# Attention and two MLPs on one core: the order of the first transfers, and new prices for the planner

## The chip, the cores and the metric

The kernel runs on one core of a Trainium2 chip. The metric is the device time of one execution in microseconds. The core has a matrix engine (TensorE, called PE in the profile; its weight loads stand under PEld), a vector engine (VectorE, DVE), a scalar engine for activations (ScalarE, ACT), GpSimd (POOL), a sync engine that mostly issues transfers (SyncE, SP), and DMA queues that the engines fill. PE writes to PSUM banks; everything else lies in SBUF or in device memory.

## The reference

Four batches of eight heads, 576 tokens, head dimension 64. The attention output is the input of a first MLP, and that of a second, gated one. All arrays are float32, but the weights come to the chip as 64-bit floats. q, k and `w_gate` are drawn some six times larger than the other inputs, so the softmax is sharp and a coarse number format would show.

```
log_f = np.log(np.clip(f, 0.0001, 1.0));  cum = np.cumsum(log_f, axis=-1)
decay = cum[:, :, :, None] - cum[:, :, None, :]
scores = np.where(causal, -1000000000.0, scale * q @ k.T + decay)
attn = softmax(scores) @ v                          # 4 x 8 x 576 x 64
x = attn.transpose(0, 2, 1, 3).reshape(2304, 512)
h = x @ w_in                                        # 512 -> 2048
x = (h * np.tanh(np.log1p(np.exp(h)))) @ w_out      # -> 512
out = (sigmoid(x @ w_gate) * (x @ w_val)) @ w_out2  # 512 -> 1536 -> 512
```

## The kernel before

**Number formats.** The MLPs run in split fp16: a value is a high and a low half, and a product is three matmuls (high-high, high-low, low-high; lines 1114 to 1116 for `w_in`, 1165 to 1167 for `w_out`). A weight tile arrives as 512 KB of raw 64-bit words. `load_w` sends it (line 712), `float32` rebuilds float32 on DVE in three integer instructions of 128 x 512 (lines 662, 666, 670), `scaled` makes the high half on ACT (line 527) or DVE (line 530), and `low_part` the low half: on DVE (line 681), or on PE with two matmuls into a bank `w_ps` (lines 687 and 688) that ACT reads out (line 690). The first MLP has 32 such tiles, n = 0 to 31: two for `win0`, then `win1` and so on, with `wout0` and the rest among them. Raw words land in parts of `xt`, or, for tiles 2 and 3, in `win5` and `win4` (`XPLACE`).

**Start.** `decay` loads the gates `f` and a matrix `carry`, clips (line 471), takes the logarithm with a sum per row on ACT (line 473), runs a small Exp, so that the Exp table is loaded (line 474), adds up earlier segments with one matmul by `carry` (line 479), and scans (line 484). The running sums go as rows into the score operands (line 490): the row `rq` beside q on SP's queue, `rk` beside k on ACT's, each in two segments. `ones` puts the rows of constants beside them (lines 426 and 428): in a score product, a row of sums beside k meets a row of constants beside q, and the other way round. `constants` loads an identity (`eyes`).

**Attention.** The first 256 queries of batch 0 run in fp32, a pair of heads at a time, four pairs p: `scores_first` (line 821, into `s_ps`), a row maximum with the mask on DVE (line 756), Exp on ACT (line 808), a diagonal of reciprocals (line 530), transposes by matmul (`t_ps`, line 847), and the product with v (line 1011). All the rest of the attention has scores of 384 to 576 columns (lines 886, 891, 953), probabilities in two fp16 halves (`pp`, lines 527 and 764), transposes by DMA (line 930), and its product with v at line 1023.

**Steps.** The first MLP goes in steps: one step is a block of 256 tokens and a group g of 256 hidden columns. `h_stream` issues a step's h matmuls into one of three `h` banks, `mish` applies the activation on ACT and DVE, which frees the bank with the low half of g (line 1087), and `y_stream` adds g times `wout` into `y_ps`. Step 0 is the first block's group 0, step 7 its group 7.

**Order.** Nothing of the order is written by hand. All the pieces are coroutines; the class `Order` runs them as a list scheduler with a clock for each engine, estimated costs, and a due time for each piece. Prices (`P_DVE`, `P_ACT`, `P_POOL`, `P_PORT`, `TAU`, `NEAR`) decide between plans on different engines; numbers such as `MISH`, `PRE0`, `B0`, `VLATE` shift due times. What it yields is a fixed instruction list for each engine. Each engine runs its list in order and waits on semaphores. In gaps that the planner expects for PE it puts matmuls by the mask into a `y_ps` bank (`fill`, line 1129), which compute nothing that is used; there are 80 of them.

Of the kernel before, what the change touches and what calls it, by code (L numbers as in the profile page):

```python
# [11 lines left out]
ACTF = mybir.ActivationFunctionType  # L12
# [24 lines left out]
DMA_LAG = 2.007  # L37
# [2 lines left out]
WP0 = 0  # L40
SLACK = 0.571
SLACK_P = 3.484
NEAR = 0.092
P_DVE = 2.396
P_ACT = 3.156
P_POOL = 1.906
P_PORT = 7.287
P_EXP = 2
TAU = 28.792
LOAD0 = 0.5  # L50
FILL0 = 1.2
FILL = 0.7
# [10 lines left out]
class Order:  # L63
# [162 lines left out]
    def run(self):  # L226
        while True:
            self.unblock()
            best = None
            for e, ops in self.ops.items():  # L230
                if ops:
                    c = self.clock[e]
                    first = min(self.begin(t, c) for t in ops) + NEAR

                    ready = [t for t in ops if self.switch(t) and t["time"] < c - PATIENCE]
                    ready = ready or [t for t in ops if self.begin(t, c) <= first]
                    t = min(ready, key=lambda t: (t["due"], t["n"]))
                    start = self.begin(t, c)
                    if e == "SP" and len(t["req"]) > 2 and t["req"][1] < 1:

                        start = max(start, self.clock["DMA"] - DMA_QUEUE)
                    if best is None or start < best[0]:
                        best = start, e, t
            if best is None:
                break
            start, e, t = best
            cold = False
            if e == "PE":
                gap, busy = max(0.0, start - self.clock[e]), 0.0
                cold = self.warm * 2.0 ** (-gap / TAU_PE) < WARM  # L250
                if self.fill and gap > FILL_MIN:

                    share = FILL if self.n_fill else FILL0
                    busy = self.fill(int(share * gap / (FILL_US * (1 + cold)))) * FILL_US * (1 + cold)
                    self.n_fill += busy > 0
                    busy = min(busy, gap)
                self.warm *= 2.0 ** (-(gap - busy) / TAU_PE)
                self.warm = 1.0 - (1.0 - self.warm) * 2.0 ** (-busy / TAU_PE)
                cold = self.warm < WARM
            self.ops[e].remove(t)  # L260
            if self.switch(t):
                self.table = t["req"][2]
            _, us, *dma = t["req"]
            if e == "PE":
                us *= 1 + cold
                self.warm = 1.0 - (1.0 - self.warm) * 2.0 ** (-us / TAU_PE)
            if e != "SP":
                dma = ()
            self.use(e, start, us)
            if self.port(t["req"]):  # L270
                self.use("PORT", start, us)
            end = start + us
            if dma:
                t["time"] = end
                self.clock["DMA"] = end = max(self.clock["DMA"], end + 0.65) + dma[0] / DMA_RATE
                end += DMA_LAG
                if len(dma) > 1:
                    self.event[dma[1]] = end
                    self.changed = True
                else:  # L280
                    t["time"] = end
            elif e == "PE":

                t["time"], t["lag"] = end, self.AFTER[e]
            else:
                t["time"] = end + self.AFTER[e]
            self.step(t, None)
        assert not self.blocked, [(t["due"], t["req"]) for t in self.blocked]
# [39 lines left out]
def attention_moe_moe_kernel(ctx, tc, qk, v, f, carry, ident, const, rows_q, rows_k, w_in, w_out, w_gate, w_val, w_out2, out):  # L328
# [37 lines left out]
    def need(*keys):  # L366
        yield ("need", keys)
# [46 lines left out]
    Q32 = SAB.rearrange("p a q h s -> p a q (h s)").bitcast(FP32)  # L414

    def constants():
        yield "SP", 0.5, 131072, "eye"
        nc.sync.dma_start(out=eyes, in_=ident)
        od.due(0)
        yield "SP", 0.5, 10000, "cq"  # L420
        nc.sync.dma_start(out=SBt[67:KB], in_=rows_q)

    def ones():

        yield "SP", 0.5, 10000, "ones_k"
        nc.sync.dma_start(out=K32[64:65].rearrange("o a q s -> o (a q s)"), in_=const[0:1])
        yield "SP", 0.5, 10000, "ones_q"
        nc.sync.dma_start(
            out=Q32[65:KF].rearrange("o a q s -> o (a q s)"), in_=const[1:2, 0:2 * NPB * 320]
        )  # L430
        yield from need("ones_k", "ones_q")
        done("ones")
# [23 lines left out]
    def decay():  # L456
        ft = words(wout[NG1 - 1], 1536, 2 * SL).bitcast(FP32)
        cum = words(wout[NG1 - 2], 1536, 2 * SL).bitcast(FP32)
        c16 = words(win[NG1 - 2], 0, 3 * SL).rearrange("p (a s) -> p a s", a=3)
        zt = words(wout[0], 0, 2 * SL).bitcast(FP32)  # L460
        tot, car, tab = (words(wout[0], 2 * SL + 2 * k, 2).bitcast(FP32) for k in range(3))
        cm = words(wout[0], 512, 256).bitcast(FP32)
        yield "SP", 0.5, 74000, "gates"
        nc.sync.dma_start(out=ft, in_=f)
        yield "SP", 0.5, 65536, "carry"
        nc.sync.dma_start(out=cm, in_=carry)
        yield from need("gates")
        yield "DVE", t_dve2(SL) + 0.2
        nc.vector.memset(zt, 0.0)
        nc.vector.memset(tab, 0.0)  # L470
        nc.vector.tensor_scalar(ft, ft, 1.0e-4, 1.0, op0=ALU.max, op1=ALU.min)
        yield "ACT", t_act(SL, 0.28)
        nc.scalar.activation(out=ft, in_=ft, func=ACTF.Ln, accum_out=tot)
        nc.scalar.activation(out=tab, in_=tab, func=ACTF.Exp, scale=0.0)
        yield from need("carry")
        (hi,) = yield from take("h")
        hp = t_ps("h", "carry_ps")[:, 0:1]
        yield "PE", 0.3
        nc.tensor.matmul(hp, lhsT=cm, rhs=tot, start=True, stop=True)
        yield "DVE", 0.13  # L480
        nc.vector.tensor_copy(car, hp)
        give("h", hi)
        yield "DVE", t_dve(SL)
        nc.vector.tensor_tensor_scan(out=cum, data0=ft, data1=zt, initial=car, op0=ALU.add, op1=ALU.add)

        for seg in range(2):
            for row, key in ((Q32[64:65], "rq"), (K32[65:KF], "rk")):
                n = min(SL, 256 - seg * SL)
                yield "SP", 0.5, 10000, (key, seg)
                (nc.scalar if key == "rk" else nc.sync).dma_start(  # L490
                    out=row.rearrange("o a q s -> o (a q) s")[:, :, seg * SL:seg * SL + n],
                    in_=cum[seg * NH:seg * NH + 2 * NPB, 0:n],
                )
        od.due(-20)
        for seg in range(1, 4):
            yield "SP", 0.5, 5000, ("cum_f", seg)
            nc.sync.dma_start(out=cum_f[:, seg * SL:(seg + 1) * SL], in_=cum[seg * NH:seg * NH + 2 * NPB])
        spawn(first_rows(), -20)
        yield from need(*[("cum_f", seg) for seg in range(1, 4)])
        od.due(0)  # L500
        yield "DVE", 3 * t_dve(SL) + 3 * t_dve2(SL)
        for j in range(3):
            nc.vector.tensor_copy(c16[:, j], cum)
            if j < 2:
                nc.vector.tensor_tensor(cum, cum, c16[:, j], op=ALU.subtract)
        for seg in range(4):
            yield "SP", 0.5, 10000, ("cum", seg)
            nc.sync.dma_start(
                out=cum_d.rearrange("j b t p s -> (b t p) j s")[:, :, seg * SL:(seg + 1) * SL],
                in_=c16[seg * NH:(seg + 1) * NH],  # L510
            )
# [52 lines left out]
    def prep_first(p, part, turn):  # L564
# [2 lines left out]
        j = qi % NQ  # L567
        for c in ((0, 1), (2, 3, 4))[part]:
            qs_t[p, c] = (SA[j], SB[j], c * 128 - c0, qi)
        yield "SP", 0.68, 512 * n, ("k32", p, part)  # L570
        nc.sync.dma_start(out=K32[0:64, :, p, c0:c0 + n], in_=qk[p, 64:128, :, c0:c0 + n])
        yield "SP", 0.68, 512 * n, ("q32", p, part)
# [123 lines left out]
    def load_w(hi, lo, src, scale, key, n):  # L696

        if n:
            yield from need(("st", 0) if n == 1 else ("rk", 1))

        if n in XPLACE:
            yield from take(turn=("wr", n))
# [6 lines left out]
        if n < NFIRST:  # L709
            od.due((-49.95, -49.5, -28.8, -27.8)[n])  # L710
        yield "SP", 0.5, 128 * 4096
        (nc.scalar if n < 2 else nc.sync).dma_start(
            out=raw.rearrange("p n t -> p (n t)").rearrange("p (a n) -> p a n", a=src.shape[1]), in_=src
        )
        od.due(due)
# [1124 lines left out]


    LEAD = 1.91
    MISH = -1.309
    YDUE = 4.818
    SPAN = 6.867
    LATE = 0.504
    SPANA = 7.667
    C4 = 1
    PRE = 0.948
    PRE0 = -3.072  # L1850
    B0 = 9.728
    WIN = 6
    WOUT = -2
    VLATE = 5.624
    FIRST = ()
    NFIRST = 4
    XPLACE = {2: win[5], 3: win[4]}
# [2 lines left out]
    for b in range(NB):  # L1860
# [14 lines left out]
        for p in range(NPB):  # L1875
# [4 lines left out]
            if b == 0 and p == 3:  # L1880
                spawn(constants(), beg)
                spawn(masks(), beg)
                spawn(ones(), beg - 1)
        for p in range(NPB):
            spawn(prep_v(b, p, ("ld", nl)), beg + p - pre + 1)
            nl += 1
# [97 lines left out]
```

## Time and profile before

| | us |
|---|---|
| Runs | 908.98, 909.6, 910.5 |
| Median of the three | 909.6 |
| The profiled execution | 911.16 |
| Its span in the profile | 909.4 |
| PE busy in it | 896.6 (99%) |
| DVE busy | 714.8 (79%) |
| ACT busy | 551.3 (61%) |
| POOL busy | 19.2 (2%) |

The span runs from the first to the last instruction of the profiled execution; that execution's own time, 911.16 us, has some 1.8 us around it. PE counts as busy while any of its pipelined matmuls is under way, so its 99% includes matmuls at half clock and the fills. The mean granted clock of PE is 0.992 of full speed.

### The profile page before, as it was taken

The page shows a single profiled execution, that of the slowest core. Times are in us where ns is not written, and L with a number is a line of the kernel's source. Part 1 is how long each engine was busy: PE and PEld are TensorE (multiplying, and loading weights), DVE is VectorE, ACT ScalarE, POOL GpSimd, SP SyncE. Part 2 cuts the span into 40 slices and gives each one's busy share as a digit, 9 for nine tenths or more (in the row PEclk, how much of TensorE's full clock was granted, in tenths as well). Part 3 has the DMA queues.
Part 4 walks back from the last instruction along what each step waited for, and adds up shares of the span by engine and source line. Part 5 has one row for each costly group of instructions (what it writes and reads, how often), then busy time and mean ns, then how long its engine had stood idle before and what let it go on. Part 6 is the DMA issues. An engine that isn't in the chain of part 4 may idle for free.

```text
span 909.4 us, 21833 instructions
## 1 busy us (share of the span) xinstructions
PE 896.6 (99%) x8907; PEld 746.8 (82%) x8907; DVE 714.8 (79%) x1688; ACT 551.3 (61%) x1075; POOL 19.2 (2%) x32
## 2 busy tenths in 40 slices
PE   7999999999999999999999999999999999999998
PEld 6647788878887888878888887777888888888986
DVE  5999999888768875796799989999959556756634
ACT  4688688887767876585444455556655453554432
POOL 0000100010000000000100000000000000100000
PEclk7999999999999999999999999999999999999999
DMA  7688968668657773544344433301000100010010
GB/s 215 178 219 179 234 206 216 135 134 168 135 94 140 123 177 82 103 93 90 97 137 140 139 116 117 116 2 47 1 1 2 48 1 1 24 36 13 2 48 25
DMA packets 149431, 91.69 MB, mean 101 GB/s; under 512 B 103785, under 2 KB 132929, under 8 KB 149328
## 3 DMA queue, kind: packets, MB, share of 16 engines
q1 hardware_dynamic: 148466, 88.97, 40.4%
q8 instruction: 70, 1.15, 0.6%
q10 hardware_dynamic: 864, 1.32, 0.4%
q14 instruction: 31, 0.25, 0.1%
HBM read 51.38 MB, written 5.37 MB: 62 GB/s over the span
## 4 chain that ended last, share of the span: by engine, by line
PE 91%; DVE 6%; DMA 1%; issue 0%; ACT 0%; SPq 0%; POOL 0%; DVEq 0%; POOLq 0%; ACTq 0%
PE bank L1474 9%; PE bank L1473 9%; PE bank L1475 9%; PE h_ps L1114 7%; PE y_ps L1165 7%; PE y_ps L1166 7%; PE y_ps L1167 7%; PE h_ps L1115 7%; PE h_ps L1116 7%; PE o_ps L1023 4%; PE o_bank L1633 3%; PE o_bank L1634 3%; PE o_bank L1632 3%; PE o_acc L1798 2%; PE o_acc L1797 2%; PE o_acc L1796 2%
## 5 line engine op out<-in xcount | busy, mean ns | idle before, releaser
L1114 PE MATMUL h_ps<-xt,win 128*128 128x256 f16 x576 | 157.5, 273 | 0.1
L1115 PE MATMUL h_ps<-xt,win 128*128 128x256 f16 x576 | 157.1, 273 | 0.6 <-DVE sm L781 0.3
L1165 PE MATMUL y_ps<-g,wout 128*128 128x256 f16 x576 | 157.2, 273 | 0.0
L1116 PE MATMUL h_ps<-xt,win 128*128 128x256 f16 x576 | 157.1, 273 | 0.0
L1167 PE MATMUL y_ps<-g,wout 128*128 128x256 f16 x576 | 156.9, 272 | 0.0
L1166 PE MATMUL y_ps<-g,wout 128*128 128x256 f16 x576 | 156.9, 272 | 0.0
L756 DVE CUSTOM_DVE_ANT_0 sp<-s_ps,mask 128x384 f32<-128x384 f32 (+4 forms) x144 | 68.0, 493 | 22.6 <-PE s_ps L891 19.1
L1480 ACT ACTIVATE bank<-bank 128x512 f32<-128x512 f32 (+1 forms) x90 | 48.5, 539 | 61.2 <-PE bank L1475 60.3
L906 ACT ACTIVATE sp<-sp,sm 128x384 f32<-128x384 f32 (+3 forms) x112 | 63.8, 570 | 24.9 <-DVE sm L756 23.7
L764 DVE SCALAR_TENSOR_TENSOR pp<-sp,sm,pp 128x512 f16<-128x512 f32 (+4 forms) x128 | 76.5, 610 | 1.4
L1114 PEld LDWEIGHTS <-win 128*128 128x128 f16 x576 | 56.3, 98 | 13.2 <-issue 3.3
L1165 PEld LDWEIGHTS <-wout 128*128 128x128 f16 x576 | 56.3, 98 | 11.2 <-issue 2.0
L1115 PEld LDWEIGHTS <-win 128*128 128x128 f16 x576 | 56.4, 98 | 9.2 <-issue 1.5
L1077 ACT ACTIVATE h_ps<-h_ps 128x512 f32<-128x512 f32 x72 | 41.4, 582 | 36.5 <-PE h_ps L1116 36.1
L1087 DVE SCALAR_TENSOR_TENSOR g<-h_ps,g 128x512 f16<-128x512 f32 x72 | 49.2, 687 | 17.8 <-ACT g L1083 17.7
L1166 PEld LDWEIGHTS <-wout 128*128 128x128 f16 x576 | 56.3, 98 | 8.0
L1116 PEld LDWEIGHTS <-win 128*128 128x128 f16 x576 | 56.3, 98 | 7.5 <-issue 0.9
L1167 PEld LDWEIGHTS <-wout 128*128 128x128 f16 x576 | 56.3, 98 | 6.6
L1730 DVE TENSOR_TENSOR v<-bank,e 128x512 f32<-128x512 f32 (+1 forms) x30 | 19.1, 638 | 43.3 <-ACT bank L1480 42.6
L1646 DVE SCALAR_TENSOR_TENSOR xt<-o_bank,xt 128x512 f32<-128x512 f32 x42 | 28.5, 689 | 30.2 <-ACT o_bank L1480 22.0
L1083 ACT ACTIVATE g<-h_ps 128x512 f16<-128x512 f32 x61 | 36.2, 595 | 23.3 <-PE y_ps L1167 22.6
L1023 PEld LDWEIGHTS <-vt 128*64 128x64 f16 x1368 | 35.1, 110 | 14.2 <-issue 12.8
(298 smaller groups left out, 2492.2 us busy)
## 6 DMA issues: line engine op xcount, KB each, us to landing
xt<-w_out SPq DMA_DIRECT2D x16, 512.0 KB
xt<-w_in SPq DMA_DIRECT2D x12, 512.0 KB
wraw<-w_gate SPq DMA_DIRECT2D x12, 512.0 KB
wraw<-w_val SPq DMA_DIRECT2D x12, 512.0 KB
wraw<-w_out SPq DMA_DIRECT2D x12, 512.0 KB
vst<-v SPq DMA_DIRECT2D x12, 320.0 KB
st<-qk SPq DMA_DIRECT2D x12, 320.0 KB
st<-qk SPq DMA_DIRECT2D x12, 256.0 KB
```

The costliest lines, as they stand in the source:

```text
L756: nc.vector.tensor_tensor_reduce(out=sp, in0=ps_ap, in1=mk, op0=ALU.add, op1=ALU.min, scale=-0.125, scalar=1.0e38, accum_out=mn,)
L764: nc.vector.scalar_tensor_tensor(lo, a, scale, hi, op0=ALU.mult, op1=ALU.subtract)
L1023: nc.tensor.matmul(o_ps[64 * hh:64 * hh + 64, col:col + n], lhsT=vv[:, jc, vl, 64 * hh:64 * hh + 64], rhs=ptt[:, k, q0:q0 + n], start=(jc ...
L1114: nc.tensor.matmul(dst, lhsT=wh, rhs=xh, start=(k == 0), stop=False)
L1115: nc.tensor.matmul(dst, lhsT=wh, rhs=xl, start=False, stop=False)
L1116: nc.tensor.matmul(dst, lhsT=wl, rhs=xh, start=False, stop=(k == KD - 1))
L1165: nc.tensor.matmul(dst, lhsT=wh, rhs=gh, start=first, stop=False, skip_group_check=True)
L1166: nc.tensor.matmul(dst, lhsT=wl, rhs=gh, start=False, stop=False, skip_group_check=True)
L1167: nc.tensor.matmul(dst, lhsT=wh, rhs=gl, start=False, stop=last, skip_group_check=True)
L1473: nc.tensor.matmul(dst, lhsT=wh, rhs=xh[:, k], start=first, stop=False, skip_group_check=True)
L1474: nc.tensor.matmul(dst, lhsT=wh, rhs=xl[:, k], start=False, stop=False, skip_group_check=True)
L1475: nc.tensor.matmul(dst, lhsT=wl, rhs=xh[:, k], start=False, stop=last, skip_group_check=True)
```

## The change

The rows of constants (`ones`) go out first, and on ACT's queue. The first weight tile is sent only when the logarithm is issued (`need("ln")`); the second moves from ACT's queue to SP's, and waits, like all later ones, for the decay rows (`("rk", 1)`). `constants`, and the q and k of pairs 2 and 3, wait for the second segment of decay rows (`("rows", 1)`). The dummy Exp is issued behind the carry matmul in the program's text. Two transfers get a shorter estimated landing time, and nine of the planner's numbers are new.

```
-NEAR = 0.092
-P_DVE = 2.396
+NEAR = 0.098
+P_DVE = 2.413
...
-P_POOL = 1.906
-P_PORT = 7.287
+P_POOL = 1.759
+P_PORT = 6.132
...
-TAU = 28.792
+TAU = 19.169
...
     def constants():
+        yield from need(("rows", 1))
         yield "SP", 0.5, 131072, "eye"
...
     def ones():
-        nc.sync.dma_start(out=K32[64:65].rearrange("o a q s -> o (a q s)"), in_=const[0:1])
+        nc.scalar.dma_start(out=K32[64:65].rearrange("o a q s -> o (a q s)"), in_=const[0:1])
...
-        nc.sync.dma_start(
+        nc.scalar.dma_start(
             out=Q32[65:KF].rearrange("o a q s -> o (a q s)"), in_=const[1:2, 0:2 * NPB * 320]
         )
...
         nc.scalar.activation(out=ft, in_=ft, func=ACTF.Ln, accum_out=tot)
-        nc.scalar.activation(out=tab, in_=tab, func=ACTF.Exp, scale=0.0)
+        done("ln")
...
         nc.tensor.matmul(hp, lhsT=cm, rhs=tot, start=True, stop=True)
+        nc.scalar.activation(out=tab, in_=tab, func=ACTF.Exp, scale=0.0)
...
+            done(("rows", seg))
...
+        if p > 1:
+            yield from need(("rows", 1))
         yield "SP", 0.68, 512 * n, ("k32", p, part)
...
         if n:
-            yield from need(("st", 0) if n == 1 else ("rk", 1))
+            yield from need(("rk", 1))
+        else:
+            yield from need("ln")
...
-        (nc.scalar if n < 2 else nc.sync).dma_start(
+        (nc.scalar if n < 1 else nc.sync).dma_start(
...
-    MISH = -1.309
+    MISH = -2.209
...
-    PRE0 = -3.072
-    B0 = 9.728
+    PRE0 = -1.767
+    B0 = 10.922
...
-    VLATE = 5.624
+    VLATE = 0
...
-                spawn(ones(), beg - 1)
+                spawn(ones(), -49.96)
```

On ACT, the first instructions before: `xt_74` and `xt_73` hold the raw words of tiles 0 and 1, `wout_91` the gates, `wout_90` the running sums, `xt_75` the rebuilt float32, `win_76` the two halves of `win0`.

```order
L712 DMA xt_74<-w_in 128x2x512
L473 ACT_TABLE_LOAD
L473 ACTIVATE wout_91,wout_84<-wout_91 128x144
L474 ACT_TABLE_LOAD
L474 ACTIVATE wout_84<-wout_84 128x1
L712 DMA xt_73<-w_in 128x2x512
L490 DMA mab<-wout_90 1x8x144
L527 ACTIVATE win_76<-xt_75 128x512
L490 DMA mab<-wout_90 1x8x112
L527 ACTIVATE win_76<-xt_75 128x512
```

The same place of the changed kernel:

```order
L427 DMA mab<-const 1x4608
L429 DMA sab<-const 1x2560
L474 ACT_TABLE_LOAD
L474 ACTIVATE wout_91,wout_84<-wout_91 128x144
L481 ACT_TABLE_LOAD
L481 ACTIVATE wout_84<-wout_84 128x1
L719 DMA xt_74<-w_in 128x2x512
L492 DMA mab<-wout_90 1x8x144
L492 DMA mab<-wout_90 1x8x112
L815 ACTIVATE wout_88,sm<-wout_88,sm 128x128 x2
```

The rows of constants stand first, tile 0 stands where tile 1 stood, the two decay rows follow each other, and the high halves of `win0` are no longer ahead of the first Exp of the softmax.

On DVE, from the scan of the running sums to the first softmax instruction (`ISA`), before:

```order
L484 SCALAR_TENSOR_TENSOR wout_90<-wout_91,wout_84 128x144
L662 TENSOR_SCALAR xt_75<-xt_74 128x512
L666 SCALAR_TENSOR_TENSOR xt_75<-xt_74,xt_75 128x512
L670 SCALAR_TENSOR_TENSOR xt_75<-xt_74,xt_75 128x512
L681 SCALAR_TENSOR_TENSOR win_76<-xt_75,win_76 128x512
L662 TENSOR_SCALAR xt_75<-xt_73 128x512
L666 SCALAR_TENSOR_TENSOR xt_75<-xt_73,xt_75 128x512
L670 SCALAR_TENSOR_TENSOR xt_75<-xt_73,xt_75 128x512
L681 SCALAR_TENSOR_TENSOR win_76<-xt_75,win_76 128x512
L756 ISA wout_88,sm<-s_ps,mask 128x128
```

The same place of the changed kernel:

```order
L486 SCALAR_TENSOR_TENSOR wout_90<-wout_91,wout_84 128x144
L667 TENSOR_SCALAR xt_75<-xt_74 128x512
L671 SCALAR_TENSOR_TENSOR xt_75<-xt_74,xt_75 128x512
L675 SCALAR_TENSOR_TENSOR xt_75<-xt_74,xt_75 128x512
L533 TENSOR_SCALAR win_76<-xt_75 128x512
L686 SCALAR_TENSOR_TENSOR win_76<-xt_75,win_76 128x512
L763 ISA wout_88,sm<-s_ps,mask 128x128
```

Tile 1 has moved behind the softmax of all four pairs (before, three pairs stood in one piece), and the high half of tile 0 is made on DVE.

On PE, at the first product of low part `w_ps` for `win4` in the changed kernel, with the step that follows it (step 2, `win_78`):

```order
L1136 MATMUL y_ps<-mask 128x256
L893 MATMUL s_ps<-mab,sab 128x512
L692 MATMUL w_ps<-xt_75,eyes 128x512
L693 LDWEIGHTS eyes
L693 MATMUL w_ps<-win_80,eyes 128x512
L893 MATMUL s_ps<-mab,sab 128x384
```

In the kernel before, the low part for which PE waited is that for `win3`, and h matmuls of step 1 (`win_77`) follow it:

```order
L1129 MATMUL y_ps<-mask 128x256
L886 MATMUL s_ps<-mab,sab 128x384
L687 MATMUL w_ps<-xt_75,eyes 128x512
L688 LDWEIGHTS eyes
L688 MATMUL w_ps<-win_79,eyes 128x512
L1114 LDWEIGHTS win_77
```

In all, PE has 93 fills instead of 80 (18 and 21 around the carry matmul instead of 24 and 23) and eleven low parts instead of nine. ACT has 15 instructions fewer, and DVE some 16 more, most of them high halves. The first y step stands later in PE's list, and the low half of g of steps 0 and 4 later in DVE's.

## Rows read from the trace of the kernel before

**Rows 1.** The page, chain that ended last: shares of the span by engine.
```profile
PE 91%; DVE 6%; DMA 1%; issue 0%; ACT 0%; SPq 0%; POOL 0%; DVEq 0%; POOLq 0%; ACTq 0%
```

**Rows 2.** Windows: length; busy by PE, PEld, DVE, ACT, POOL; clock; DMA share; GB/s.
```profile
13.93:21.70 7.77, 7.77 (x27) 6.14 (x27) 4.76 (x30) 5.55 (x24) 0.00 (x0) 0.50 1.02 295
21.70:58.50 36.80, 33.49 (x238) 21.45 (x235) 36.19 (x107) 27.80 (x63) 0.00 (x0) 0.93 0.68 185
58.50:85.08 26.58, 26.47 (x202) 17.34 (x200) 24.79 (x65) 21.45 (x44) 0.00 (x0) 1.00 0.87 210
85.08:909.40 824.32, 819.83 (x8394) 694.78 (x8391) 642.66 (x1475) 492.08 (x941) 18.11 (x26) 1.00 0.38 91
```

**Rows 3.** Timeline, all engines, 0 to 14 us: start, duration, engine, line, [idle before].
```profile
1.42 5.30 PE L1129 MATMUL y_ps<-mask 128*128 128x256 bf16 x24 [1.42 <-POOL mask L436]
...
3.97 0.40 ACTq L712 DMA_DIRECT2D xt<-w_in  x1
...
4.39 1.28 ACT L474 ACT_TABLE_LOAD   x1
...
5.68 0.20 ACT L474 ACTIVATE wout<-wout 128x1 f32<-128x1 f32 x1
...
6.51 0.35 PE L479 MATMUL carry_ps<-wout 128*128 128x1 f32 x2
...
7.71 1.23 ACTq L490 DMA_DIRECT2D mab<-wout  x1
...
9.49 0.64 ACTq L490 DMA_DIRECT2D mab<-wout  x1
...
10.75 0.42 DVE L662 TENSOR_SCALAR xt<-xt 128x512 int32<-128x512 int32 x1
...
13.93 0.28 DVE L756 CUSTOM_DVE_ANT_0 wout<-s_ps,mask 128x128 f32<-128x128 f32 x1
```

**Rows 4.** Chain of the first 60 us, in order of time: start, duration, what.
```profile
9.74 2.95 DMA sab<-const
```

**Rows 5.** Timeline of PE, 12 to 86 us.
```profile
12.82 7.42 PE L821 MATMUL s_ps<-mab,sab 66*128 66x128 f32 x24 [3.43 <-DMA sab<-const]
...
25.59 1.48 PE L821 MATMUL s_ps<-mab,sab 66*128 66x128 f32 x8
...
50.43 1.53 PE L687 MATMUL w_ps<-xt,eyes 128*128 128x512 f32 x2 [1.96 <-DVE xt L670]
...
59.48 1.02 PE L687 MATMUL w_ps<-xt,eyes 128*128 128x512 f32 x2
60.34 0.38 PE L688 MATMUL w_ps<-win,eyes 128*128 128x512 f16 x1
60.55 0.27 PE L1114 MATMUL h_ps<-xt,win 128*128 128x256 f16 x1
60.66 0.27 PE L1115 MATMUL h_ps<-xt,win 128*128 128x256 f16 x1
...
85.08 0.27 PE L1114 MATMUL h_ps<-xt,win 128*128 128x256 f16 x1
```

**Rows 6.** Windows around the ends of two stretches at low clock.
```profile
23.00:24.00 1.00, 1.00 (x8) 0.85 (x6) 1.00 (x4) 0.00 (x0) 0.00 (x0) 0.65 1.00 371
...
52.00:54.00 2.00, 2.00 (x6) 0.85 (x4) 1.82 (x6) 1.64 (x6) 0.00 (x0) 0.50 0.95 351
...
55.00:58.00 3.00, 3.00 (x45) 1.87 (x40) 3.00 (x7) 2.62 (x7) 0.00 (x0) 1.00 0.50 169
```

**Rows 7.** Timeline of DVE near 51 us.
```profile
50.90 0.42 DVE L662 TENSOR_SCALAR xt<-xt 128x512 int32<-128x512 int32 x1
51.24 0.69 DVE L1087 SCALAR_TENSOR_TENSOR g<-h_ps,g 128x512 f16<-128x512 f32 x1
51.84 0.68 DVE L666 SCALAR_TENSOR_TENSOR xt<-xt,xt 128x512 int32<-128x512 int32 x1
52.44 0.55 DVE L756 CUSTOM_DVE_ANT_0 sp<-s_ps,mask 128x384 f32<-128x384 f32 x1
```

More of the change, by code (lines that the diff above doesn't have):

```diff
@@ L275, in run @@
                 self.clock["DMA"] = end = max(self.clock["DMA"], end + 0.65) + dma[0] / DMA_RATE
-                end += DMA_LAG
+                end += dma[2] if len(dma) > 2 else DMA_LAG
                 if len(dma) > 1:
@@ L462, in decay @@
         cm = words(wout[0], 512, 256).bitcast(FP32)
-        yield "SP", 0.5, 74000, "gates"
+        yield "SP", 0.4, 74000, "gates", 1.0
         nc.sync.dma_start(out=ft, in_=f)
-        yield "SP", 0.5, 65536, "carry"
+        yield "SP", 0.4, 65536, "carry", 1.0
         nc.sync.dma_start(out=cm, in_=carry)
```

## The prediction

> **What bounds the kernel now.** I read the chain that ended last first: 91% of it is TensorE (PE) and 6% VectorE (DVE) [rows 1]. Then the windows, cut at 85.08 us, where PE begins the sixth of the first MLP's h steps (step 5, counting from 0) [rows 2, 5]. Behind that cut PE is busy 819.83 of 824.32 us at a granted clock of 1.00, its level of 2.4 GHz: nothing but less PE work, or starting earlier, can shorten that part. Ahead of it PE is not the bound: between 21.7 and 58.5 us DVE is busy 36.19 of 36.80 us while PE is busy 33.49, part of it at the low clock, part with fill matmuls that compute nothing.
>
> So I keep one account: clock time minus useful PE work. Useful work is counted from the order of instructions, each kind with the distance of one start to the next: 0.11 us for an fp16 matmul of 256 columns (60.55 to 60.66), 0.86 for an fp32 one of 512 columns (59.48 to 60.34), so 0.65 for 384, 0.43 for 256 and 0.215 for 128, and 1.07 for a whole low part on PE (59.48 to 60.55) [rows 5]. Ahead of step 5 the kernel before has scores 17.2 us, transposes 5.0, attention times v 8.7, 120 h and 24 y matmuls 15.7, nine low parts 9.7: 56.3 us. **85.08 - 56.3 = 28.7 us have gone to other things** by then, and almost nothing is lost later. The change can only move this 28.7 and the useful total.
>
> The start, in the timeline [rows 3]: 24 fills run from 1.42 to 6.51, 0.212 us each. The carry matmul stands behind them; 1.20 us after it, at 7.71, the rows of the decay sum are sent. ScalarE (ACT) sends the second of its two at 9.49 only, because a conversion stands in between. The ones rows go last, at 9.74, and land 2.95 us later [rows 4]. DVE meanwhile converts two weight tiles, and the first softmax runs at 13.93. The 24 score matmuls of three pairs take 7.42 us at a granted clock that falls to 0.50, the level of 1.2 GHz [rows 2, 5]; the eight of the fourth pair, at full clock, take 1.48 [rows 5].
>
> **The change, part by part.**
>
> *Six fills fewer ahead of the carry matmul* (24 to 18): 6 x 0.212 = 1.3 us. Matmul at 1.42 + 18 x 0.212 = 5.2, decay rows sent at 5.2 + 1.2 = 6.4.
>
> *Ones rows first on ACT, decay rows together.* The ones rows leave at about 0.73 us, when nothing else uses that queue, and cover is ample: they must land before 10 us. ACT's second decay row now follows the first, which occupied its queue 1.23 us [rows 3]: sent at 7.7, landed, by the 2.95 us of the ones row, at 10.7 at the latest. Scores can start at 9.6 to 10.7 instead of 12.82.
>
> *First weight tile.* In ACT's order it now stands behind logarithm, table load and dummy Exp. In the kernel before tile 1 stood there, and was issued at 3.97, although the Exp ahead of it ran at 5.68 [rows 3]: ACT's queue sends a transfer without waiting for work ahead of it to end, only for its semaphores. I take the same 3.97 for tile 0. It lands no sooner than the small ones rows, 2.95 us, and no later than tile 1, whose conversion at 10.75 shows no wait, 6.8 us. To 2.95 add 512 KB at 295 GB/s (1.8 us) [rows 2] and something for q and k ahead of it: 5.0, so 9.0 us (bounds 6.9 and 10.8). Conversion is now wholly on DVE: 0.34 + 0.60 + 0.60 [rows 7], 0.36 for the high part and 0.60 for the low, 2.5 us. **First softmax at 11.5** instead of 13.93, and only one tile converted ahead of it. The ends of the range are 10.1 (scores at 9.6 plus two narrow matmuls) and 13.3.
>
> On ScalarE the Trainium skill speaks against this: "ScalarE: Activation LUTs", section "What ACT_TABLE_LOAD costs", gives 1283 ns for a load and about 1380 ns of drain at each switch of tables. The trace agrees on the load (1.28 us) and shows no drain: the load ends at 4.39 + 1.28 = 5.67 and the Exp starts at 5.68 [rows 3]. By the page a transfer that did wait for the Exp would leave at 7.3 instead of 5.9; by the row that I use it waits for neither.
>
> *Later q, k and weight tiles on SP.* Tile 1 now comes after all eight q and k transfers and is converted behind four pairs' softmax, 7.5 us of DVE work after 11.5, at 19 us. SP sends it eighth after 6.4; at the 0.6 us that I allow for each (ACT's queue held one for 1.23 [rows 3]), at about 11. That leaves 8 us where the bound above needs 6.8 at most, so it costs nothing; without that cover, its lateness in full.
>
> *The new order of the middle* (the prices). It decides which DVE work must be done before PE can go on. PE's last hold by DVE is the start of h step 7: its PSUM bank comes free with the low half of g of step 4, moved far back. Ahead of that in DVE's order, from the first softmax: 21 conversions 31.7 us, softmax 16.1, probabilities 11.7, eight low parts 4.8, Mish 4.2, v 3.7, diagonals 3.1, attention output 2.7, sums and reciprocals 5.7, rest 3.6: 87.3 us, each kind by its distance in the trace of before, as [rows 7] show for three. To it come DVE's own waits. Before, it lost 26.58 - 24.79 = 1.8 us between 58.5 and 85.08 [rows 2]; bounds 0 and 2.6 (about 0.8 more to 100 us by the same share), value 1.0. So step 7 starts at 11.5 + 87.3 + 1.0 = 99.8 us. Useful PE work ahead of it: scores 19.2, transposes 4.8, times v 11.0, 168 h and 96 y matmuls 28.9, eleven low parts 11.8: 75.6. **Not useful: 99.8 - 75.6 = 24.2 us**, 4.5 less than 28.7. The 13 extra fills lie inside this, in gaps that DVE leaves.
>
> *Two more low parts on PE*: 2 x 1.07 = 2.1 us more of useful work, in full. In exchange ACT loses some 15 instructions and DVE gains as many. Behind 440 us both orders are the same but for names, and DVE has slack behind step 5 (642.66 of 824.32 us busy [rows 2]).
>
> **Sum:** -4.5 + 2.1 = -2.4 us. Against the profiled execution's own 911.16 that gives 908.8; that execution is 1.6 above the median of 909.6, so the median comes to **907.2 us**.
>
> **Rivals.**
>
> *Better still.* The first tile lands at 8.5 and DVE never waits: 11.0 + 87.3 - 75.6 = 22.7, so -6.0 + 2.1 = -3.9: 905.7. For it speaks that tile 0 no longer shares the DMA engines with tile 1. Against: DVE lost time wherever it waited for PE before.
>
> *The low clock stays at the start.* Before, PE idled 3.43 us ahead of the scores, and the clock fell to 0.50 soon after. Now the 21 fills behind the carry matmul end between 7.9 and 10.0 us (0.11 to 0.212 each), so the idle time is 0 to 2.8 us; ahead of the low part at 50.43 an idle time of 1.96 was followed by 0.50 too [rows 5, 6]. Then a pair's scores take 7.42 / 3 = 2.5 instead of 1.48 us, the fourth pair ends at about 20 instead of being there when DVE reaches it at 17.2, and DVE, which now has four softmaxes in a row, is held some 2.7 us. -2.4 + 2.7 = +0.3: 909.9, no change.
>
> *The queue does wait for the Exp*, so that the change delays the tile that it means to bring early: sent at 5.9, first softmax at 13.4, -2.4 + 1.9 = -0.5: 909.1. The 3.97 speaks against it. By the page's drain it would be 1.4 more, 910.5.
>
> *Slower: low clock in the middle.* PE waits for DVE's conversion of tile 8 near 52 us with few fills ahead. Before, the clock was 0.50 at 52 to 54 us and 1.00 from 55 on [rows 6]. If it stayed down as long as at the start, some 10 us (0.50 from 13.93 on [rows 2], 0.65 as the mean of 23 to 24 [rows 6]), PE would do 5 us less work in just the stretch where DVE needs its scores: -2.4 + 5.0 = +2.6, 912.2. It decides from 4.2 us lost, some 8.4 us at half clock. Against it: the stretch before was short, and PE is dense behind it.
>
> **How the numbers follow.** Chances: the forecast 0.50, better 0.10, low clock at the start 0.20, queue waits 0.07, slower 0.10, anything else 0.03. The forecast alone spans 905.3 to 909.2 (first softmax 10.5 to 12.5, DVE's waits 0 to 2.0). To hold 8 in 10 the range takes in the better case and the low clock at the start, 904.8 to 911.0; most of the slower case is left out. 0.2%, about what a measurement of this kernel tells from none, is 1.8 us. Faster than 907.8: two thirds of the forecast, the better case and a little of the rest, 0.50. Slower than 911.4: 0.13. Same: 0.37.
>
> **What would show it.** Right: carry matmul near 5.2; tile 0 issued by ACT near 4; scores from about 10 with 1.48 us a pair; first softmax near 11.5; h step 7 near 99.8, preceded by a wait of PE for DVE's low half of g; PE idle below 5 us behind it. Wrong: tile 0 issued after 5.7; score matmuls at 2.5 us a pair; a granted clock of 0.50 for many us near 52; DVE with more than 3 us of idle time between its first softmax and 100 us; or PE idle again after 100 us, because the early lead meets late weights.

## The result, and the profile after

The changed kernel takes 915.26 us (median of 15 runs, 912.39 to 917.91), the kernel before beside it 911.03 (15 runs, 908.64 to 913.04): a ratio of 1.0051 with an interval of [1.0041, 1.0061], so it is **slower by 4 to 5 us**. The forecast was 907.2, with a range from 904.8 to 911.0. The profiled execution has a span of 913.5 us against 909.4. The executions of the changed kernel spread with their mean granted clock: the one at 0.996 took 912.39 us, the five at 0.991 took 916.2 to 917.9; the profiled one stands at 0.994. All medians and ratios below leave out one stray execution each of `a_cap9` (1870 us) and of `b_fill_memlo` (3230 us).

First the steps of the start that the forecast named. The timeline of the changed kernel (start, duration, engine, line, what, idle time ahead and what ended it), against [rows 3] and [rows 5]:

```profile
1.42 4.02 PE L1136 MATMUL y_ps<-mask 128*128 128x256 bf16 x18 [1.42 <-POOL mask L437]
...
3.88 0.41 ACTq L719 DMA_DIRECT2D xt<-w_in  x1
...
4.30 1.28 ACT L481 ACT_TABLE_LOAD   x1
...
5.23 0.39 PE L480 MATMUL carry_ps<-wout 128*128 128x1 f32 x2
5.48 2.45 PE L1136 MATMUL y_ps<-mask 128*128 128x256 bf16 x21
5.60 0.20 ACT L481 ACTIVATE wout<-wout 128x1 f32<-128x1 f32 x1
...
6.47 1.42 ACTq L492 DMA_DIRECT2D mab<-wout  x2
...
9.14 0.43 DVE L667 TENSOR_SCALAR xt<-xt 128x512 int32<-128x512 int32 x1 [2.70 <-DMA xt<-w_in]
...
9.56 1.55 PE L828 MATMUL s_ps<-mab,sab 66*128 66x128 f32 x8 [1.63 <-DMA sab<-wout]
...
12.12 0.28 DVE L763 CUSTOM_DVE_ANT_0 wout<-s_ps,mask 128x128 f32<-128x128 f32 x1
12.68 8.05 PE L828 MATMUL s_ps<-mab,sab 66*128 66x128 f32 x24 [1.57 <-DVE sm L763]
...
13.94 0.29 DVE L763 CUSTOM_DVE_ANT_0 wout<-s_ps,mask 128x128 f32<-128x128 f32 x1 [0.62 <-PE s_ps L828]
...
15.64 0.42 DVE L763 CUSTOM_DVE_ANT_0 wout<-s_ps,mask 128x256 f32<-128x256 f32 x1 [1.20 <-PE s_ps L828]
...
18.20 0.42 DVE L763 CUSTOM_DVE_ANT_0 wout<-s_ps,mask 128x256 f32<-128x256 f32 x1 [0.90 <-PE s_ps L828]
...
23.02 0.42 DVE L863 COPY pt<-t_ps 128x256 f32<-128x256 f32 x1 [1.47 <-PE t_ps L854]
...
58.01 1.10 PE L692 MATMUL w_ps<-xt,eyes 128*128 128x512 f32 x2 [2.67 <-DVE xt L675]
...
106.33 0.68 DVE L1094 SCALAR_TENSOR_TENSOR g<-h_ps,g 128x512 f16<-128x512 f32 x1
...
106.48 0.60 PE L1136 MATMUL y_ps<-mask 128*128 128x256 bf16 x4
...
107.07 0.27 PE L1121 MATMUL h_ps<-xt,win 128*128 128x256 f16 x1
```

Down to 9.14 everything came as forecast: tile 0 leaves at 3.88 while the Exp ahead of it in ACT's order starts at 5.60, the carry matmul runs at 5.23, the decay rows leave at 6.47. The first pair's eight score matmuls take 1.55 us. Then comes what the forecast did not have: the second pair waits **1.57 us for DVE**. Its scores go into a PSUM bank that is free only when the first softmax (12.12) has read the first pair's. The 24 score matmuls behind that wait take 8.05 us, 2.7 a pair, and DVE, which should have run four softmaxes in a row, now waits three times for scores (0.62, 1.20 and 0.90 us) and once for the transposes behind them (1.47), 4.2 us in all. The h step 7 starts at 107.07, where the forecast had 99.8. The low half of g that frees its bank ends at 106.33 + 0.68 = 107.01; PE comes to the four fills ahead of the step at 106.48, and has not waited since 58.01. So DVE and PE are nearly level there.

The windows of the changed kernel (columns as in [rows 2]):

```profile
12.00:13.00 1.00, 0.32 (x1) 0.33 (x2) 1.00 (x8) 0.56 (x3) 0.00 (x0) 0.64 0.84 189
...
12.25:12.50 0.25, 0.00 (x0) 0.00 (x0) 0.25 (x3) 0.06 (x1) 0.00 (x0) 0.54 0.72 147
...
14.00:22.00 8.00, 8.00 (x27) 6.31 (x27) 5.30 (x34) 5.65 (x25) 0.00 (x0) 0.50 1.00 359
22.00:23.00 1.00, 1.00 (x9) 0.96 (x7) 0.00 (x0) 0.32 (x2) 0.00 (x0) 0.74 0.84 159
23.00:24.00 1.00, 1.00 (x11) 0.97 (x10) 0.95 (x5) 0.00 (x0) 0.00 (x0) 1.00 0.87 287
...
55.00:60.00 5.00, 2.33 (x20) 1.23 (x15) 4.90 (x15) 4.05 (x9) 0.00 (x0) 1.00 0.22 60
...
107.07:913.50 806.43, 801.50 (x8175) 678.87 (x8173) 626.13 (x1430) 475.00 (x904) 23.06 (x23) 1.00 0.36 87
```

The granted clock falls near 12.25 us, while PE still waits for the bank, and is 0.50, the level of 1.2 GHz, for some 10 us. In the middle it stays at 1.00, although PE idles there too, 2.67 us ahead of the low part at 58.01: the rival with the low clock near 52 us did not occur in this execution (whether it did in those with a lower mean clock, no trace shows). Behind step 7 PE idles 806.43 - 801.50 = 4.9 us in all, much as before behind its step 5 [rows 2]. Over the whole span no other wait of PE behind its first instruction is longer than 0.5 us.

By my account (clock time minus useful work, counted in both traces as in the forecast) the changed kernel leads by 4.9 us at 50 us and by 0.7 at 100 us. So the early lead was there and was given back.

### The profile page after: what moved, and what is told of

Its sections match the earlier page's. It is cut to its first block, busy times and chain, and to the rows that moved or that the text cites. A ratio compares the mean times of both kernels' runs of the same rounds, so it can differ in the third digit from the quotient of the medians.

```text
span 913.5 us, 21880 instructions
## 1 busy us (share of the span) xinstructions
PE 900.3 (99%) x8926; PEld 747.6 (82%) x8926; DVE 719.4 (79%) x1703; ACT 548.6 (60%) x1062; POOL 26.1 (3%) x34
## 4 chain that ended last, share of the span: by engine, by line
PE 79%; DVE 7%; DMA 2%; ACT 1%; issue 1%; SPq 0%; ACTq 0%; DVEq 0%
PE bank L1480 8%; PE bank L1481 8%; PE bank L1482 8%; PE y_ps L1172 6%; PE h_ps L1121 6%; PE y_ps L1173 6%; PE y_ps L1174 6%; PE h_ps L1122 6%; PE h_ps L1123 6%; PE o_ps L1030 3%; PE o_bank L1641 3%; PE o_bank L1640 3%; PE o_bank L1639 3%; PE s_ps L897 1%; PE s_ps L898 1%; PE o_acc L1805 1%
## 5 line engine op out<-in xcount | busy, mean ns | idle before, releaser
L1653 DVE SCALAR_TENSOR_TENSOR xt<-o_bank,xt 128x512 f32<-128x512 f32 x42 | 28.4, 689 | 31.5 <-ACT o_bank L1487 23.6
```

## Experiments

Each kernel ran in turns with the kernel before on the same chip; the ratios are to that one. The main theory (theory 1): the bank wait brings the low clock, and that costs the gain. Its rivals: the two additional low parts on PE, the order of the middle that the new numbers make, and DVE's own work. To fill a gap I used fill matmuls, which compute nothing and change no other instruction's order.

**Both gaps filled, and the same cure for the kernel before.** `a_fill` is the changed kernel with 13 fills behind the carry matmul and 13 behind the first pair's scores:

```diff
         nc.tensor.matmul(hp, lhsT=cm, rhs=tot, start=True, stop=True)
+        od.fill(13)
...
+            if p == 0 and gi == 1:
+                od.fill(13)
             spawn(soft(gi, pst, tag, si), od.cur["due"])
```

`b_fill` is the kernel before with `od.fill(27)` behind its carry matmul.

> The changed kernel with 13 more fills behind the carry matmul and 13 between the scores of the first and the second pair; every other instruction and its order are the same on all engines. Theory 1 (the clock at the start): the changed kernel wins 1.8 us up to the first softmax and loses it because PE idles twice (1.63 and 1.57 us) around the first scores, falls to 0.50 and holds DVE. Then scores take some 1.5 us a pair, DVE does not wait for them (2.7 + 1.5 us now), the low part of tile 8 (58.0 now) starts by 55, and the time falls by 2 to 3 us against the changed kernel: 1 to 2 us above the kernel before (ratio about 1.002). Rival (what PE has to wait for in the middle is set by DVE's order, or by the two more low parts): the start gets faster, the end moves by less than 1 us, ratio about 1.004 to 1.005.

> The kernel before with 27 more fills behind the carry matmul, which cover PE's 3.43 us of idle time ahead of the scores; all else the same, in the same order. Theory 1: scores at full clock (1.5 us a pair instead of 2.5), DVE ahead by some 3 us from 20 us on, 2 us off the end: ratio about 0.998. Rival: from 58 us on PE and not DVE is the bound in this order, so that the end moves by less than 1 us: ratio 0.999 to 1.000.

Measured: `a_fill` 910.75 us, ratio 1.0003 [0.9993, 1.0014]; `b_fill` 908.69, ratio 0.9978 [0.9964, 0.9993]. PE's timeline of `a_fill`, then its windows:

```profile
10.04 1.55 PE L829 MATMUL s_ps<-mab,sab 66*128 66x128 f32 x8
11.42 1.58 PE L1139 MATMUL y_ps<-mask 128*128 128x256 bf16 x13
13.14 4.45 PE L829 MATMUL s_ps<-mab,sab 66*128 66x128 f32 x24
...
54.35 1.68 PE L693 MATMUL w_ps<-xt,eyes 128*128 128x512 f32 x2 [2.78 <-DVE xt L676]
...
104.71 0.27 PE L1124 MATMUL h_ps<-xt,win 128*128 128x256 f16 x1
```

```profile
15.00:20.00 5.00, 5.00 (x38) 4.23 (x37) 4.93 (x33) 4.90 (x23) 0.00 (x0) 1.00 1.03 380
...
55.00:60.00 5.00, 5.00 (x18) 2.64 (x17) 5.00 (x12) 1.97 (x5) 0.00 (x0) 0.69 1.03 223
```

The second pair still starts near 13 us, but the three pairs take 4.45 instead of 8.05 us, at a clock of 1.00. The whole excess of the changed kernel, 1.0051 - 1.0003 = 0.48% or **4.4 us, goes with it**. The kernel before had a low clock at its start too, behind another gap: the 3.43 us ahead of its first scores. The three pairs that took it 7.42 us [rows 5] take 1.55 + 2.89 in `b_fill`; that is worth 1.9 us, and `b_fill` beats both kernels. With these gaps filled on both sides the change still costs 910.75 - 908.69 = 2.1 us, on the same chip. Four of the nine executions of `b_fill` have a mean clock of only 0.994 or 0.995; among those at 0.998 or more the medians are 910.4 and 907.7, so 2.7 us.

**Which gap: one at a time, and the bank itself.** `a_fill_gap1` has only the first `od.fill(13)`, `a_fill_gap2` only the second. `a_bank` has no more fills than the changed kernel; the second pair gets a bank of its own:

```diff
-            pst = t_ps(tag, "s_ps")
+            pst = t_ps("h" if p == 1 else tag, "s_ps")
```

> The changed kernel with the 13 fills behind the carry matmul alone; the 1.57 us of idle time between the first and the second pair's scores stays. If the first idle time (1.63 us) is what the clock falls for: no 0.50 in 12 to 22 us, and nearly all of a_fill's gain, ratio about 1.001. If both together count, or the second alone: the clock falls as in the changed kernel, ratio about 1.005. In the changed kernel the first pair's scores behind the first idle time still ran at full clock (1.55 us), which speaks for the second.

> The changed kernel with the 13 fills between the first and the second pair's scores alone; the 1.63 us of idle time ahead of the first scores stays. If the second idle time decides: no 0.50, ratio about 1.001. If the first, or both: ratio 1.003 to 1.005, with the clock low from about 13 us or earlier.

> The changed kernel with the second pair's scores written to banks of the h pool, which lie free at that time, instead of banks that the first pair's softmax must read out first. No fills are added and every instruction keeps its place. If this wait alone makes the clock fall: PE goes from the first pair to the second without idling, no 0.50 in 12 to 22 us, and the gain of a_fill_gap2, ratio 1.001 to 1.003. If the 1.63 us ahead of the first scores suffice for the low clock: ratio 1.004 to 1.005 as in the changed kernel.

Measured: `a_fill_gap1` 914.50 us, 1.0044 [1.0027, 1.0060]; `a_fill_gap2` 912.40, 1.0022 [1.0010, 1.0035]; `a_bank` 912.41, 1.0018 [1.0004, 1.0033]. PE's timelines of `a_fill_gap1`, of `a_fill_gap2` and of `a_bank`, in this order:

```profile
9.91 1.49 PE L829 MATMUL s_ps<-mab,sab 66*128 66x128 f32 x8
12.97 7.33 PE L829 MATMUL s_ps<-mab,sab 66*128 66x128 f32 x24 [1.56 <-DVE sm L764]
```

```profile
8.76 1.82 PE L828 MATMUL s_ps<-mab,sab 66*128 66x128 f32 x8 [0.45 <-DMA sab<-wout]
10.42 1.58 PE L1138 MATMUL y_ps<-mask 128*128 128x256 bf16 x13
11.84 4.35 PE L828 MATMUL s_ps<-mab,sab 66*128 66x128 f32 x24
```

```profile
9.88 2.86 PE L828 MATMUL s_ps<-mab,sab 66*128 66x128 f32 x16 [1.10 <-DMA sab<-wout]
13.00 1.82 PE L828 MATMUL s_ps<-mab,sab 66*128 66x128 f32 x8 [0.26 <-DVE sm L763]
15.22 1.58 PE L828 MATMUL s_ps<-mab,sab 66*128 66x128 f32 x8 [0.40 <-DVE sm L763]
```

The window of `a_fill_gap1`, then that of `a_bank`, from 15 to 20 us:

```profile
15.00:20.00 5.00, 5.00 (x17) 4.19 (x16) 3.74 (x25) 3.98 (x18) 0.00 (x0) 0.50 1.01 354
```

```profile
15.00:20.00 5.00, 4.78 (x38) 4.15 (x39) 4.90 (x31) 5.00 (x24) 0.00 (x0) 1.00 1.00 352
```

With the first gap closed and the bank wait left, the clock is 0.50 and the time hardly moves. With the bank wait gone, by fills or by another bank, it is 1.00 in the profiled executions and most of the excess goes (2.6 and 3.0 of the 4.6 us), although a first gap of 0.45 and 1.10 us is left. So **the bank wait of 1.57 us is enough to bring the low clock**. That the gap ahead of the scores does not bring it by itself is shown for 1.10 us only: in these two executions that gap was shorter than the changed kernel's 1.63, though neither edit touches it.

`a_fill_gap2` and `a_bank` stay some 1.5 us above `a_fill`. Their executions differ in clock: the six of `a_bank` with a mean of 0.998 or more, the profiled one among them, took 909.9 to 912.2 us, level with `a_fill`; the six below took 912.6 to 916.1. So in half of them the clock still fell somewhere, for the first gap or in the middle; no trace shows which. The other way round, one execution of `a_fill_gap1` kept 0.998, and took 910.97.

**The two additional low parts on PE.** `a_cap9` lets the planner put only nine there and plan anew. `a_swap2` does the tenth and eleventh on DVE, in their places and with nothing else moved; `a_fill_swap2` is the same on top of `a_fill`:

```diff
+        if len(on_pe) > 9:
+            yield plan[1]
+            nc.vector.scalar_tensor_tensor(lo, w, scale, hi, op0=ALU.mult, op1=ALU.subtract)
+            give(tag, ai)
+            return
         nc.tensor.matmul(acc, lhsT=eye, rhs=w, start=True, stop=False)
```

`a_fill_skip2` has a memset in place of the DVE operation in `a_fill_swap2`.

> The changed kernel with at most nine low parts on PE, as before, instead of eleven; the same order up to the tenth of them, near 80 us, and another one behind it, since the planner goes on from there. Theory 2 (the two more low parts are paid in full, because PE is the bound behind 60 us): 2.1 us less than the changed kernel, ratio about 1.0025. Rival: DVE, which then makes both low parts (1.2 us), is what PE waits for near 100 us, so nothing or at most 1 us is won: ratio 1.004 to 1.005.

> The changed kernel with its tenth and eleventh low part made on DVE (one instruction each, where ACT would have read the bank) instead of on PE; all other instructions in the same order. Theory 2 (PE is the bound behind 60 us, so the two more low parts are paid in full): 2.1 us less than the changed kernel, ratio to the kernel before about 1.002 to 1.003. Rival (DVE still decides when step 7 can start, and gets 1.2 us more): 0 to 1.2 us more than the changed kernel, ratio 1.005 to 1.0065.

> The same two low parts on DVE, together with the 13 + 13 fills of a_fill. If both causes (clock at the start, two more low parts on PE) add up: 2 us below a_fill, ratio about 0.998, level with b_fill. If DVE decides behind step 2: 0 to 1.2 us above a_fill, ratio 1.000 to 1.0015.

> a_fill without its tenth and eleventh low part on PE; a memset on DVE of some 0.2 us stands in their place, so these two low parts are missing from the output. 2.1 us less PE work, 0.4 us more on DVE, all else in the same order. If the two products are what a_fill has more to do than b_fill, and PE is the bound: 2 us below a_fill, ratio about 0.998. If the order of DVE's work decides, so that PE would only wait longer: less than 1 us, ratio 0.9995 to 1.000.

Measured: `a_cap9` 918.02 us, 1.0079 [1.0062, 1.0096]; `a_swap2` 916.12, 1.0061 [1.0045, 1.0076]; `a_fill_swap2` 913.04, 1.0028 [1.0014, 1.0042]; `a_fill_skip2` 912.16, 1.0015 [1.0003, 1.0028]. None is faster than the kernel that it was made from, though PE has 2.1 us less to do. `a_cap9` says the least, since its order is another one behind the tenth (PE idles 3.5 us from 120 to 200). PE's waits of `a_fill_skip2` show why:

```profile
PE h_ps L1133 <- DVE xt L1067: 0.9, 1, 0.9
PE s_ps L971 <- DVE sm L772: 0.9, 1, 0.9
PE h_ps L1132 <- DVE g L1105: 0.9, 1, 0.9
PE y_ps L1184 <- DVE wout L689: 0.6, 1, 0.6
```

Of these, the last three are not among the waits of `a_fill`: PE arrives earlier and waits for DVE instead. So taking the two low parts off PE wins nothing in this order: at those places they lie in time that PE has.

**DVE's work.** `a_fill_diag` and `b_fill_diag` move 16 diagonals of the first scores from DVE to ACT (`scaled(..., act=True)`). `a_fill_memlo` and `b_fill_memlo` put `nc.vector.memset(lo, 0.0)` in place of DVE's low parts.

> a_fill with the 16 diagonals of the first attention part made on ACT instead of DVE, at the same places: 3.1 us less DVE work ahead of 30 us, all else in the same order. Theory 4 (with the clock held up, DVE's work still decides when PE can go on, up to step 12 near 130 us; two low parts moved to DVE in a_fill_swap2 cost 2.3 us): 2 to 3 us below a_fill, ratio about 0.997 to 0.998. Rival (DVE is held by ACT instead, or PE is the bound): no gain, ratio 1.000 to 1.001.

> b_fill with the same 16 diagonals on ACT. Theory 4 for the order of before: DVE has 3.1 us less to do ahead of 30 us, but PE is bound by its own work from about 50 us in that run and not by DVE, so at most 1 us: ratio 0.997 to 0.998. If DVE decides there too: 2 to 3 us, ratio about 0.995. If ACT holds the transposes up: ratio above 0.999.

> a_fill with the low halves that DVE makes of the first MLP's weights left out: each is replaced by a memset of the same half, which takes DVE some 0.2 instead of 0.6 us, so about 0.4 us less, eight times ahead of step 7 and 21 times in all. The output lacks these low parts. If DVE's work decides in a_fill up to step 7 and beyond: step 7 starts 2 to 3 us sooner and the time falls by 2 to 3 us, ratio about 0.997 to 0.998. If PE or transfers decide: less than 1 us.

> The same omission in b_fill: about 0.4 us less DVE work for each of its low halves on DVE. The output lacks these low parts. If the order of before leaves DVE room, so that the 2.3 us between a_fill and b_fill are DVE work on the path in one order and not in the other: less than 1 us, ratio 0.997 to 0.998. If DVE decides there as much: 2 to 3 us, ratio about 0.995.

Measured: `a_fill_diag` 911.46 us, 1.0006 [0.9994, 1.0018]; `b_fill_diag` 908.62, 0.9979 [0.9964, 0.9995]; `a_fill_memlo` 909.86, 0.9987 [0.9976, 0.9998]; `b_fill_memlo` 907.30, 0.9968 [0.9950, 0.9987]. The diagonals change nothing in either kernel; DVE's freed time ahead of 25 us turned into waits (from 20 to 25 us it is busy 3.69 us instead of 4.93), so this pair tells nothing on the middle. Cheaper low parts give 0.16% and 0.10%, less than the intervals can part. Both kernels gain about as little, so nothing here shows that these low parts explain the 2.1 us between them.

**The clock in the middle.** `a_fill` has 0.69 at 55 to 60 us, behind a wait of 2.78 us. `a_fill2` puts 20 more fills ahead of that low part.

> a_fill with 20 more fills ahead of the low part of tile 8, where PE idles 2.8 us and the clock falls to 0.83 over 50 to 60 us. If the low clock there costs PE time that is not won back: 1 us below a_fill, ratio about 0.999. If DVE decides (theory 4): no change, ratio 1.000.

Measured: 910.19 us, 0.9993 [0.9982, 1.0004]. Its window there:

```profile
55.00:60.00 5.00, 5.00 (x24) 2.75 (x23) 5.00 (x12) 2.42 (x5) 0.00 (x0) 1.00 1.04 236
```

The clock stays up and step 7 starts at 103.23 instead of 104.71, but the median time is not measurably another. `a_fill` itself kept a mean clock of 1.000 in five of its twelve executions, which took 909.5 to 910.4 us; the other seven, the profiled one among them, took 910.6 to 913.0, with medians 1.5 us apart. So this low clock does not always come, and seems to cost some 1.5 us when it does.

**Numbers and transfers apart.** `a_oldnum` is the changed kernel with the nine planner numbers of before; `b_newnum` the kernel before with the nine new ones.

> The changed kernel's transfers and waits with the planner's nine numbers of before (nine low parts on PE). Theory 3 (the numbers, and so the order of the middle, cost the time): the transfers alone are no slower than the kernel before, ratio 0.998 to 1.000. Theory 1: the scores come earlier but at the low clock here too, so the transfers alone win nothing: ratio 0.999 to 1.001. Rival (the transfers cost the time): ratio above 1.003.

> The kernel before with the nine new numbers alone, its transfers as before (seven low parts on PE). With the old numbers the new transfers took 922 us. If the numbers bring the loss by themselves, this one is slower too, ratio above 1.003. If they do harm only with the new transfers, or the other way round: ratio 1.000 or below.

Measured: `a_oldnum` 922.20 us, 1.0115 [1.0098, 1.0132]; `b_newnum` 925.33, 1.0163 [1.0138, 1.0187]. Each half alone is worse than both together. The stretch that loses most, of `a_oldnum` and then of `b_newnum`:

```profile
120.00:200.00 80.00, 74.79 (x775) 62.10 (x775) 66.77 (x181) 59.54 (x129) 2.10 (x3) 0.96 0.71 161
```

```profile
200.00:440.00 240.00, 234.90 (x2718) 195.07 (x2716) 179.96 (x545) 170.04 (x330) 6.69 (x14) 0.99 0.62 121
```

PE idles 5.2 us from 120 to 200 in the one and 5.1 us from 200 to 440 in the other. The changed kernel idles 0.14 us in each of these stretches, the kernel before 0.00. These are 5 of the 7 us by which `a_oldnum` is slower than the changed kernel, and 5 of the 14.5 by which `b_newnum` is slower than the kernel before. That the order of the middle fits one start and not another is how I read it; the two runs show only that neither half does well alone.

## Why the prediction was wrong, point by point

**Right.** The transfers: carry matmul 5.23 (forecast 5.2), tile 0 sent at 3.88 (near 4) and converted from 9.14 (landing 9.0), decay rows at 6.47 (6.4). The rival in which the queue waits for the Exp did not occur. The first softmax ran at 12.12 instead of 11.5, mostly because the five conversion steps took 9.14 to 12.12, 3.0 us and not 2.5.

**The step that failed: "DVE's own waits", 1.0 us.** Step 7 starts where the sum has it, behind DVE's low half of g. But 12.12 + 87.3 + waits = 107.07 leaves **7.6 us** for the waits. DVE's windows from the first softmax to step 7, in the changed kernel, in `a_fill` and in `b_fill`, split them:

```profile
12.12:107.07 94.95, 90.75 (x704) 62.64 (x704) 88.81 (x262) 70.44 (x154) 1.91 (x5) 0.95 0.80 208
```

```profile
12.58:104.71 92.13, 87.82 (x707) 59.66 (x706) 89.19 (x262) 70.47 (x155) 1.92 (x5) 0.98 0.81 215
```

```profile
13.13:98.63 85.50, 79.46 (x654) 53.92 (x653) 82.22 (x244) 67.94 (x150) 2.01 (x4) 1.00 0.88 216
```

In the changed kernel DVE idles 94.95 - 88.81 = **6.1 us** instead of 1.0, and its work takes 1.5 more than 87.3. Of the idle time 4.2 us are the four waits up to 23.02. Two of the forecast's own signs of being wrong were there: more than 3 us of idle time of DVE, and 2.7 us a pair of scores. I had bounded the term by 0 and 2.6 from a stretch of before behind 58.5 us, where all buffers were in flow; the changed work stood at the start, where one pair's softmax frees the next pair's bank. [rows 2] showed what I left out: from 13.93 to 21.70 DVE idled 7.77 - 4.76 = 3.0 us in the kernel before as well. In `a_fill` DVE idles 92.13 - 89.19 = 2.9. So 3.2 us of the term go with the low clock at the start, and the 2.9 that are left would still have been above my bounds.

**The rival with the right mechanism had the wrong place and price.** "The low clock stays at the start" looked at the gap ahead of the scores, and took the other pairs as running back to back. The gap between the pairs sufficed. It priced the held DVE at 2.7 us, which came to "no change"; the four waits were 4.2. Taking the bank wait away is worth 2.6 to 3.0 us, filling both gaps 4.4.

**The reference was not constant in the account.** I set the new step 7 against 28.7 us of time not useful at step 5 of before. At its own step 7 (102.75, useful 71.1) the kernel before has 31.7 by the same account; the changed one has 107.07 - 75.6 = 31.5. Instead of -4.5 this term is about -0.2. But PE did not lose those 3.0 us between step 5 and step 7 of before:

```profile
85.08:102.75 17.67, 17.36 (x197) 12.92 (x194) 16.88 (x48) 13.42 (x24) 2.85 (x6) 1.00 0.85 221
```

It idles 0.3 us there and runs no fills. Most of the 3.0 is a wrong price. The 32 score matmuls of 288 columns stand behind step 5 of before and ahead of both steps 7. The forecast has 19.2 - 17.2 = 2.0 us for them; in the trace of before the next instruction starts 1.02 to 1.13 us behind each eight, 4.3 in all:

```profile
91.65 1.19 PE L953 MATMUL s_ps<-mab,sab 66*64 66x288 f32 x8
92.78 0.28 PE L1165 MATMUL y_ps<-g,wout 128*128 128x256 f16 x1
```

With 4.3 in its place the forecast would have been 2.3 us lower still, and further off.

**Two more low parts, +2.1 us.** Useful work did grow by two low parts. But "in full" is wrong as a price: without them PE waits for DVE (`a_fill_skip2`).

**"Almost nothing is lost later."** By my account the changed kernel loses some 2.2 us more than before behind step 7: 4.1 in spans, less 2.1 of useful work, less the -0.2. One wait accounts for 0.5 (a bank of the output stage, for ACT). The rest I could not assign to a row.

The miss in spans is 6.5 us (+4.1 instead of -2.4): 0.6 for the first softmax, 6.6 for the waits and the larger work of DVE, -3.0 for the reference, and 2.2 behind step 7. That last one is what remains, so it adds up by construction.

**Open.** Why the change costs 2.1 us with the gaps filled on both sides. Taking the two low parts off PE does not win it back, and cheaper low parts on DVE help both kernels by about as little (0.16% and 0.10%). The traces show where it arises: ahead of step 7 DVE has 89.19 us of work in `a_fill` and 82.22 in `b_fill`, and idles about as long in both (2.9 and 3.3). So step 7 comes 6.1 us later (104.71 against 98.63), though the first softmax came earlier (12.58 against 13.13), and only some 4.5 us of that is useful PE work, 2.1 of it the two added low parts. The order of the middle is what is left as the cause, argued and not shown.

## What to carry over

Where a start runs into a few banks, price the wait of each group for its predecessor's reader, and not only the first transfer: a gap of 1.57 us cost this kernel some 3 us, and with the gap ahead of it 4.4, through the matrix engine's clock. Look at the granted clock of the first 30 us before tuning an order there, and fill the gaps first: 27 fills won 0.2% in the old kernel (0.9978), which the whole reordering did not. When a change has two halves, such as new transfers and new planner numbers, measure them together too: here each half alone was slower than both. And read the clock of every execution, not only of the profiled one: here executions of the same kernel differ by 5 to 6 us with it.

## What the runs showed of the hardware

- The idle time alone does not tell whether the clock falls. In the changed kernel 2.67 us ahead of 58.01 left it at 1.00, and 1.57 us ahead of 12.68 were followed by some 10 us at 0.50; in `a_fill` 2.78 us ahead of 54.35 were followed by 0.69 as the mean of 55 to 60. A gap has to be priced both ways.
- ACT's queue sent tile 0 at 3.88, 1.72 us ahead of the Exp that stands before it in ACT's order (5.60). The load of the table took 1.28 us and the Exp followed at once (4.30 + 1.28 = 5.58). On this the Trainium skill, "ScalarE: Activation LUTs", section "What ACT_TABLE_LOAD costs", gives the same load and about 1380 ns of drain beside it; the trace of the changed kernel shows no drain either.
